# GLA recurrence and squared-ReLU MLP in one kernel: which queue loads blocks 3 and 4, and the order of the opening

## Chip, core and metric

One core of one Trainium2 chip. The metric is the device time of one execution in microseconds (us). Differences are judged by medians of runs on the same chip.

## The reference

For each of 4 batches and 8 heads a state of 48 x 48 is carried over 768 steps: it decays by alpha, takes the outer product of k and v, and is read with q. The heads' outputs, side by side, are the 384 columns of x (3072 rows), which go through a squared-ReLU layer of width 2048.

```python
for t in range(S):
    state = alpha[:, :, t, :, None] * state + einsum('bhd,bhe->bhde', k[:, :, t], v[:, :, t])
    y[:, :, t] = einsum('bhd,bhde->bhe', q[:, :, t], state)
x = y.transpose(0, 2, 1, 3).reshape(B * S, H * D)
r = maximum(x @ w_in, 0)
out = (s * (r * r) + b) @ w_out
```

## The kernel before

The rows of x are cut into 24 blocks of 128 (six for each batch). Block n needs four loads (alpha, k, q, v; 192 KB each, in runs of 192 bytes), and then passes these steps. The names are those of the kernel's functions, and blocks are counted from 0, so that the "third and fourth block" are numbers 2 and 3.

- `ln` (L203, ScalarE): logarithm of alpha.
- `cum` (L210, TensorE; L221 and L222, ScalarE): cumulated sum by a triangular matrix, then two exponentials, the inverse decay and the decay. For the first five blocks a third, small exponential (L224) gives the block's total decay. From block 6 on the total decay goes through DRAM instead (`decay`, L230 and L232): one row is written out and read back, by SyncE's DMA queue.
- `vcast` (L206, GpSimd): v to bf16.
- `qk` (L238, L239, VectorE, also DVE): the products k times inverse decay and q times decay.
- `tr` (L244, TensorE; L249, VectorE): transposes of both, and their copy out of PSUM.
- `amat` (L259, TensorE; L267, VectorE): q times k for each head, written to the two PSUM tiles `a_ps`, and then masked.
- `yp` (L278, L287, L298, TensorE; L305, ScalarE): y from the carried state and from the block itself, the block's share of the next state, and y to bf16. `st` (L334 VectorE, L339 and L343 GpSimd) brings the state forward.
- `xt` (L312, TensorE; L318, ScalarE): y transposed, the layer's input.
- `mp(g, u)` (L365, TensorE): a quarter u of the hidden units of block g, 12 matmuls. It writes one of two PSUM tiles `h_ps` in turn, or `o_ps` where (g, u) is listed in `h_in_o` (L351). `rl` (L379, ScalarE) is its relu, `sq` (L386, VectorE) its square. `mr` is mp and rl; `m` is mp, rl and sq.
- `o(g, u)` (L402, TensorE): a quarter of the second matmul, four matmuls that add up over u = 0 to 3. Block 1 adds up in the first tile of `a_ps`, block 2 in the second one, all others in `o_ps`. Behind u = 3 the sum of an early block is copied to a store in SBUF (L411, ScalarE), since the bias is not ready yet.

The weights come by DMA as four quarters each of w_in (768 KB) and w_out. `win(i)` turns a quarter of w_in to bf16 (L154 ScalarE, L156 VectorE). `wout(i)` does so for w_out: quarters 1 and 3 on VectorE (L160), quarter 2 on ScalarE (L168), quarter 0 half and half. `colsum` (L175, L177, VectorE) adds up w_out for the bias.

Nothing is scheduled by the compiler. Each engine runs its instructions in the order in which the program issues them, and that order is a list sorted by position: the opening (L512 to L527) is written out by hand, from `(ln, 0)` to the attention matmuls of block 4; later blocks have positions by formula (L541 on). `busy` (L191) puts matmuls without use on TensorE in the opening; they write `o_ps`.

The loads are issued ahead of the list: blocks 0 and 1 by SyncE, then the quarters of w_in with two loads each of blocks 2 and 3 between, then w_out, then blocks 4 to 7. Two more loads each of blocks 2 and 3 are issued by ScalarE, in its own DMA queue, where the list has `early` (L492).

Of the kernel before, what the change touches and what calls it, by code (L numbers as in the profile page):

```python
# [14 lines left out]
def kernel(  # L15
# [12 lines left out]
    nc = tc.nc  # L28
# [88 lines left out]
    def src(t, n):  # L117
        b, c = n // NCH, n % NCH
        return t[b, :, c * C : (c + 1) * C, :].rearrange("h s d -> s h d")

    def load_a(n, eng=None):
        (eng or nc.sync).dma_start(out=al_sb[n % NLD], in_=src(alpha, n))

    def load_q(n, eng=None):
        (eng or nc.sync).dma_start(out=q_sb[n % NLD], in_=src(q, n))

    def load_k(n, eng=None):
        (eng or nc.sync).dma_start(out=k_sb[n % NLD], in_=src(k, n))

    def load_v(n, eng=None):  # L130
        (eng or nc.sync).dma_start(out=v_sb[n % NLD], in_=src(v, n))
# [8 lines left out]
    def load_w_in(i):  # L140
        cols = slice(i * d_ff // 4, (i + 1) * d_ff // 4)
        nc.sync.dma_start(
            out=w_in_st[:, :, cols], in_=moe_w_in[:, cols].rearrange("(t r) f -> r t f", t=KT)
        )
# [203 lines left out]
    nrelu = [0]  # L348


    h_in_o = {(1, 3), (2, 2)}  # L351
    h_of = {}

    def mp(g, u):
# [94 lines left out]
    quarter = d_ff // 4  # L449
    load_w_in(0)  # L450
    load_w_in(1)
    load_q(2)
    load_v(2)
    load_w_in(2)
    load_w_in(3)
    load_q(3)
    load_v(3)
    for j in range(0, NJ, 4):
        load_w_out(j, j + 4)
    for n in range(4, NLD):  # L460
# [17 lines left out]
    def at(pos, fn, *args):  # L478
        events.append((pos, len(events), fn, args))
# [10 lines left out]
            cast_w_out(4 * i, 4 * i + 4, i == 2)  # L490

    def early(n):  # L492
        load_a(n, nc.scalar)
        load_k(n, nc.scalar)

    def win(i):
        cast_w_in(i * quarter, (i + 1) * quarter, int(i < 3))
# [14 lines left out]
    for pos, what in enumerate(  # L512
        [
            (ln, 0), (vcast, 0), (cum, 0), (qk, 0), (spread,), (busy, 3), (tr, 0), (busy, 1), (ln, 1), (vcast, 1), (amat, 0),
            (cum, 1), (early, 2), (busy, 3), (yp, 0), (qk, 1), (st, 0), (busy, 1), (tr, 1), (xt, 0), (busy, 2), (amat, 1),
            (win, 0), (win, 1), (busy, 5), (yp, 1), (mr, 0, 0), (st, 1), (busy, 1), (xt, 1), (ln, 2), (early, 3), (mr, 0, 1),
            (sq, 0, 0), (cum, 2), (sq, 0, 1), (m, 1, 0), (mr, 1, 1), (vcast, 2), (qk, 2), (sq, 1, 1), (busy, 4), (tr, 2),
            (win, 2), (busy, 3), (amat, 2), (busy, 1), (mr, 0, 2), (mr, 1, 2), (yp, 2), (win, 3), (st, 2), (sq, 0, 2),
            (sq, 1, 2), (busy, 2), (ln, 3), (xt, 2), (mr, 0, 3), (cum, 3), (mr, 1, 3), (vcast, 3), (qk, 3), (mr, 2, 0),
            (sq, 0, 3), (mr, 2, 1), (mr, 2, 2), (tr, 3), (sq, 1, 3), (mr, 2, 3), (sq, 2, 0), (wout, 0), (amat, 3),  # L520
            (busy, 3), (o, 0, 0), (yp, 3), (sq, 2, 1), (st, 3), (sq, 2, 2), (sq, 2, 3), (wout, 1), (o, 1, 0), (xt, 3),
            (o, 2, 0), (m, 3, 0), (m, 3, 1), (wout, 2), (o, 0, 1), (o, 1, 1), (colsum, 1), (ln, 4), (m, 3, 2), (m, 3, 3),
            (wout, 3), (o, 2, 1), (cum, 4), (o, 0, 2), (vcast, 4), (qk, 4), (o, 1, 2), (o, 2, 2), (colsum, 2), (o, 0, 3),
            (o, 1, 3), (o, 2, 3), (tr, 4), (o, 3, 0), (amat, 4),
        ]
    ):
        at(0.1 * pos, *what)  # L527
# [63 lines left out]
```

## Time and profile before

| what | value |
|---|---|
| median of 3 runs (range) | 197.93 us (197.66 to 198.06) |
| profiled execution | 197.71 us |
| its span, first to last instruction | 195.9 us |
| mean granted TensorE clock | 1.00 |
| VectorE, ScalarE, GpSimd busy | 151.6, 118.6, 62.1 us |
| TensorE idle until its first matmul | 4.5 us |
| DMA, mean over the span | 155 GB/s |
| transposes of blocks 2, 3, 4 start | 22.14, 30.88, 45.56 us |
| attention matmuls of block 4 start | 47.03 us |

A line of a timeline gives the start in us from the span's beginning, the duration, the engine, the line of the kernel, output and inputs with their shapes, how many instructions are merged, and in brackets how long the engine had been idle and what ended that. Matmuls are pipelined: a merged row lasts longer than the distance to the next one. "issue" in the chain is time in which the engine waited for nothing that the profile shows.

### The profile page before, as it was taken

Reading aid. Unit: us, or ns where it says so; the run is one execution under the profiler, and the core shown is the slowest. Engines: PE = TensorE matmul, PEld = TensorE weight load, DVE = VectorE, ACT = ScalarE, POOL = GpSimd, SP = SyncE. Lnnn points to the kernel's source line nnn. Section 1 sums busy time; section 2 is a strip of 40 time slices with the busy share of each in tenths; the row PEclk is TensorE's granted clock in tenths of the full one; section 3 lists DMA queues with packets and bytes.
Section 4 is the critical chain, followed back from the end, with each engine's and each line's share of the span. In section 5 each row is a group of like instructions: output and inputs, shape, how many; then the busy total and the mean of one; then the engine's idle time right before and its main releaser. Section 6 shows DMA issues by size and latency. Waiting matters only on the chain.

```text
span 195.9 us, 6122 instructions
## 1 busy us (share of the span) xinstructions
PE 183.2 (94%) x2441; PEld 143.4 (73%) x2441; DVE 151.6 (77%) x296; ACT 118.6 (61%) x243; POOL 62.1 (32%) x96
## 2 busy tenths in 40 slices
PE   0979798999899999999999999999999999999994
PEld 0547486775767678778878877887877877877783
DVE  5486779886577597988977996989887999998532
ACT  3256486565767566676586676675675666654650
POOL 5143141511310074524500650531701752652000
PEclk9999999999999999999999999999999999999999
DMA  6999999999999546845968569549849563332202
GB/s 122 191 338 225 325 268 372 208 191 192 174 195 160 111 78 94 158 85 85 202 124 141 96 93 161 100 88 253 164 122 208 103 147 124 85 120 84 93 31 80
DMA packets 113454, 30.33 MB, mean 155 GB/s; under 512 B 106627, under 2 KB 111890, under 8 KB 113426
## 3 DMA queue, kind: packets, MB, share of 16 engines
q1 hardware_dynamic: 109262, 29.15, 73.5%
q10 hardware_dynamic: 4164, 0.79, 2.8%
q8 instruction: 19, 0.31, 0.7%
q14 instruction: 9, 0.07, 0.1%
HBM read 25.19 MB, written 4.74 MB: 153 GB/s over the span
## 4 chain that ended last, share of the span: by engine, by line
PE 76%; DMA 8%; DVE 7%; ACT 4%; issue 3%; SPq 0%; ACTq 0%; DVEq 0%
PE h_ps L365 26%; PE o_ps L402 26%; PE ct_ps L244 6%; DMA k_sb<-in_k_dram 6%; PE a_ps L259 3%; PE a_ps L402 3%; PE y_ps L287 2%; ACT r_sb L379 2%; DVE qkT L249 2%; PE ct_ps L210 2%; PE h_ps L312 2%; DMA al_sb<-in_alpha_dram 2%; DVE qb_sb L239 2%; PE y_ps L278 1%; PE p_ps L298 1%
## 5 line engine op out<-in xcount | busy, mean ns | idle before, releaser
L379 ACT ACTIVATE r_sb<-h_ps 128x512 bf16<-128x512 f32 x94 | 55.8, 597 | 39.1 <-PE h_ps L365 37.4
L365 PE MATMUL h_ps<-xd_all,w_in_bf 128*128 128x128 bf16 x1128 | 74.6, 219 | 0.7 <-ACT xd_all L318 0.3
L365 PEld LDWEIGHTS <-w_in_bf 128*128 128x128 bf16 x1152 | 69.2, 98 | 7.2 <-issue 1.1
L402 PE MATMUL o_ps<-w_out_bf,gt_all 128*128 128x384 bf16 x336 | 68.5, 326 | 0.3 <-ACT w_out_bf L168 0.2
L386 DVE TENSOR_TENSOR gt_all<-r_sb 128x512 bf16<-128x512 bf16 x96 | 45.0, 480 | 26.5 <-ACT r_sb L379 25.8
L339 POOL TENSOR_TENSOR sd_sb<-t_sb,blast 48x192 bf16<-48x192 f32 x40 | 21.6, 539 | 100.2 <-DVE t_sb L334 62.7
L402 PEld LDWEIGHTS <-gt_all 128*128 128x128 bf16 x368 | 32.5, 98 | 16.3 <-issue 0.5
L206 POOL CAST v_bf<-v_sb 128x384 bf16<-128x384 f32 x24 | 18.0, 756 | 16.0 <-DMA v_sb<-in_v_dram 13.2
L318 ACT ACTIVATE xd_all<-h_ps 128x384 bf16<-128x384 bf16 x24 | 11.7, 489 | 14.8 <-PE h_ps L312 14.8
L343 POOL TENSOR_TENSOR sc_sb<-t_sb,blast 112x384 f32<-112x384 f32 x16 | 20.2, 1265 | 1.3
L249 DVE COPY qkT<-ct_ps 112x1024 bf16<-112x1024 bf16 x24 | 16.4, 683 | 4.2 <-PE ct_ps L244 2.9
L238 DVE TENSOR_TENSOR kb_sb<-k_sb,bi_sb 128x384 bf16<-128x384 f32 x24 | 14.8, 617 | 5.3 <-ACT bi_sb L221 3.7
L239 DVE TENSOR_TENSOR qb_sb<-q_sb,b_sb 128x384 bf16<-128x384 f32 x24 | 16.9, 706 | 1.5 <-ACT b_sb L222 1.5
L267 DVE TENSOR_TENSOR am_a<-a_ps,mask 128x512 bf16<-128x512 f32 x24 | 16.4, 682 | 1.8 <-PE a_ps L259 1.8
L267 DVE TENSOR_TENSOR am_b<-a_ps,mask 128x512 bf16<-128x512 f32 x24 | 16.3, 679 | 0.0
L203 ACT ACTIVATE la_sb<-al_sb 128x384 bf16<-128x384 f32 x24 | 12.4, 517 | 4.0 <-DMA al_sb<-in_alpha_dram 4.0
L221 ACT ACTIVATE bi_sb<-ct_ps 128x384 f32<-128x384 f32 x24 | 11.7, 487 | 4.1 <-PE ct_ps L213 2.3
L244 PEld LDWEIGHTS <-qb_sb 128*112 128x112 bf16 x96 | 8.0, 132 | 7.5 <-DVE qb_sb L239 6.5
L305 ACT ACTIVATE y_bf<-y_ps 128x384 bf16<-128x384 f32 x24 | 11.7, 487 | 2.3 <-PE y_ps L287 2.3
L222 ACT ACTIVATE b_sb<-ct_ps 128x384 f32<-128x384 f32 x24 | 11.9, 494 | 1.6 <-DMA row_dr<-b_sb 1.6
L210 PE MATMUL ct_ps<-la_sb,U_bf 128*128 128x384 bf16 x24 | 8.0, 333 | 4.7 <-ACT la_sb L203 4.7
L244 PE MATMUL ct_ps<-ident,qb_sb 128*112 128x128 bf16 x96 | 10.1, 228 | 2.1 <-DVE qb_sb L239 1.9
(66 smaller groups left out, 191.1 us busy)
## 6 DMA issues: line engine op xcount, KB each, us to landing
q_sb<-in_q_dram SPq DMA_DIRECT2D x24, 192.0 KB, 4.1
v_sb<-in_v_dram SPq DMA_DIRECT2D x24, 192.0 KB, 4.2
al_sb<-in_alpha_dram SPq DMA_DIRECT2D x22, 192.0 KB, 3.0
k_sb<-in_k_dram SPq DMA_DIRECT2D x22, 192.0 KB, 4.1
w_in_st<-in_moe_w_in_dram SPq DMA_DIRECT2D x4, 768.0 KB
w_out_st<-in_moe_w_out_dram SPq DMA_DIRECT2D x4, 768.0 KB
out_dram<-w_in_st SPq DMA_DIRECT2D x13, 192.0 KB, 3.6
out_dram<-out_sb SPq DMA_DIRECT2D x10, 192.0 KB, 3.5
```

Source lines behind the costliest of these rows:

```text
L206: nc.gpsimd.tensor_copy(out=v_bf[n % 3], in_=v_sb[n % NLD])
L238: nc.vector.tensor_tensor(out=kb_sb[n % 3][:, :, 0:48], in0=k_sb[n % NLD], in1=bi_sb[n % 2], op=ALU.mult)
L239: nc.vector.tensor_tensor(out=qb_sb[n % 2][:, :, 0:48], in0=q_sb[n % NLD], in1=b_sb[n % 2], op=ALU.mult)
L244: nc.tensor.transpose(out=t_ps[0:112, x, p, :], in_=t.rearrange("a h d -> a (h d)")[:, 128 * p : 128 * p + 112], identity=ident,)
L249: nc.vector.tensor_copy(out=qkT_sb[n % 2][0:112].rearrange("a x p t -> a (x p t)"), in_=t_ps[0:112].rearrange("a x p t -> a (x p t)"),)
L267: nc.vector.tensor_tensor(out=am_sb[e][n % 2], in0=a_ps[e], in1=mask4, op=ALU.mult)
L339: nc.gpsimd.tensor_tensor(out=sd[r, :, d], in0=t1_sb[r, :, d], in1=bl[r].to_broadcast([48, NP, 48]), op=ALU.mult)
L343: nc.gpsimd.tensor_tensor(out=sc_sb[0:112], in0=t1_sb[0:112], in1=bl[0:112].to_broadcast([112, NP, 96]), op=ALU.mult)
L365: nc.tensor.matmul(out=hp[:, jj * N : (jj + 1) * N], lhsT=w_in_bf[:, kk, 128 * j : 128 * (j + 1)], rhs=xd_sb[g][:, kk, 0:N], start=(kk == ...
L379: nc.scalar.activation(out=rs, in_=h_of.pop((g, u)), func=AF.Relu)
L386: nc.vector.tensor_tensor(out=gt_sb[g][:, u * 512 : (u + 1) * 512], in0=rs, in1=rs, op=ALU.mult)
L402: nc.tensor.matmul(out=op[:, 0:d_model], lhsT=gt_sb[g][:, j * N + t * C : j * N + (t + 1) * C], rhs=w_out_bf[:, j, :], start=(j == 0), sto ...
```

## The change

Three things change. SyncE loads alpha and k of blocks 2 and 3 where it loaded q and v; ScalarE's `early` loads q and v where it loaded alpha and k. The opening's list has another order from `(early, 3)` on: `cum` and `qk` of block 2 and 3 stand ahead of some relus (`rl`) and squares (`sq`), for which mp, rl and sq are now listed apart; w_out's casts, the column sum and the last `o` quarters stand elsewhere; 28 filler matmuls in place of 29. The two groups that write `o_ps` are (2, 0) and (0, 3), formerly (1, 3) and (2, 2).

```diff
-    h_in_o = {(1, 3), (2, 2)}
+    h_in_o = {(2, 0), (0, 3)}
...
-    load_q(2)
-    load_v(2)
+    load_a(2)
+    load_k(2)
     load_w_in(2)
     load_w_in(3)
-    load_q(3)
-    load_v(3)
+    load_a(3)
+    load_k(3)
...
     def early(n):
-        load_a(n, nc.scalar)
-        load_k(n, nc.scalar)
+        load_q(n, nc.scalar)
+        load_v(n, nc.scalar)
...
-            (win, 0), (win, 1), (busy, 5), (yp, 1), (mr, 0, 0), (st, 1), (busy, 1), (xt, 1), (ln, 2), (early, 3), (mr, 0, 1),
-            (sq, 0, 0), (cum, 2), (sq, 0, 1), (m, 1, 0), (mr, 1, 1), (vcast, 2), (qk, 2), (sq, 1, 1), (busy, 4), (tr, 2),
-            (win, 2), (busy, 3), (amat, 2), (busy, 1), (mr, 0, 2), (mr, 1, 2), (yp, 2), (win, 3), (st, 2), (sq, 0, 2),
-            (sq, 1, 2), (busy, 2), (ln, 3), (xt, 2), (mr, 0, 3), (cum, 3), (mr, 1, 3), (vcast, 3), (qk, 3), (mr, 2, 0),
-            (sq, 0, 3), (mr, 2, 1), (mr, 2, 2), (tr, 3), (sq, 1, 3), (mr, 2, 3), (sq, 2, 0), (wout, 0), (amat, 3),
-            (busy, 3), (o, 0, 0), (yp, 3), (sq, 2, 1), (st, 3), (sq, 2, 2), (sq, 2, 3), (wout, 1), (o, 1, 0), (xt, 3),
-            (o, 2, 0), (m, 3, 0), (m, 3, 1), (wout, 2), (o, 0, 1), (o, 1, 1), (colsum, 1), (ln, 4), (m, 3, 2), (m, 3, 3),
-            (wout, 3), (o, 2, 1), (cum, 4), (o, 0, 2), (vcast, 4), (qk, 4), (o, 1, 2), (o, 2, 2), (colsum, 2), (o, 0, 3),
-            (o, 1, 3), (o, 2, 3), (tr, 4), (o, 3, 0), (amat, 4),
+            (win, 0), (win, 1), (busy, 5), (yp, 1), (mr, 0, 0), (st, 1), (busy, 1), (xt, 1), (ln, 2), (early, 3), (mp, 0, 1),
+            (sq, 0, 0), (cum, 2), (rl, 0, 1), (mr, 1, 0), (vcast, 2), (qk, 2), (sq, 0, 1), (mr, 1, 1), (busy, 1), (tr, 2),
+            (sq, 1, 0), (busy, 3), (amat, 2), (win, 2), (busy, 5), (yp, 2), (st, 2), (busy, 1), (xt, 2), (mr, 0, 2), (win, 3),
+            (mp, 1, 2), (ln, 3), (rl, 1, 2), (mp, 2, 0), (sq, 1, 1), (cum, 3), (rl, 2, 0), (vcast, 3), (sq, 0, 2), (mr, 2, 1),
+            (qk, 3), (sq, 1, 2), (mr, 2, 2), (mr, 0, 3), (tr, 3), (mr, 1, 3), (sq, 2, 0), (mr, 2, 3), (amat, 3), (sq, 2, 1),
+            (wout, 0), (busy, 2), (yp, 3), (st, 3), (o, 0, 0), (xt, 3), (sq, 0, 3), (sq, 1, 3), (o, 1, 0), (sq, 2, 2),
+            (sq, 2, 3), (m, 3, 0), (wout, 1), (o, 2, 0), (m, 3, 1), (m, 3, 2), (wout, 2), (o, 0, 1), (m, 3, 3), (o, 1, 1),
+            (ln, 4), (wout, 3), (colsum, 1), (o, 2, 1), (cum, 4), (o, 0, 2), (vcast, 4), (qk, 4), (o, 1, 2), (o, 2, 2),
+            (tr, 4), (o, 1, 3), (colsum, 2), (o, 2, 3), (amat, 4), (o, 0, 3), (o, 3, 0),
```

## The prediction

> **What bounds the kernel now.** I read the page first, then the granted clock by stage, then the chain of waits, then each engine's timeline from 16 to 70 us. The profiled execution took 197.71 us: a span of 195.9 us and 1.8 us around it. The median of the three runs is 197.93 us; the sum is made against 197.71 and 0.2 us is added at the end.
>
> From the page: TensorE (PE) is busy 94% of the span; in the second fence line each digit is a slice of 4.9 us, and behind the first five PE has two eights and, at the end, a 4; all else is 9. The DMA row is at 9 for slices 2 to 13, to about 64 us.
>
> ```profile
> PE 183.2 (94%) x2441; PEld 143.4 (73%) x2441; DVE 151.6 (77%) x296; ACT 118.6 (61%) x243; POOL 62.1 (32%) x96
> ...
> PE   0979798999899999999999999999999999999994
> ...
> DMA  6999999999999546845968569549849563332202
> ```
>
> Part of that opening PE time is filler (`busy`). So in the opening the bound is read from what PE waits for. The timelines give three waits on inputs: block 2's v, block 3's alpha and block 3's k.
>
> ```profile
> 19.85 0.50 POOL L206 CAST v_bf<-v_sb 128x384 bf16<-128x384 f32 x1 [0.43 <-DMA v_sb<-in_v_dram]
> ...
> 26.87 0.52 ACT L203 ACTIVATE la_sb<-al_sb 128x384 bf16<-128x384 f32 x1 [0.20 <-DMA al_sb<-in_alpha_dram]
> ...
> 29.06 1.30 DVE L238 TENSOR_TENSOR kb_sb<-k_sb,bi_sb 128x384 bf16<-128x384 f32 x1 [1.41 <-DMA k_sb<-in_k_dram]
> ```
>
> (start, duration, engine, line, then in brackets the idle time and what ended it.) After 36 us PE has almost no gap until the first decay row, which sits in SyncE's queue behind all loads up to block 10. The chain of waits shows that place:
>
> ```profile
> 64.26 2.69 DMA row_dr<-b_sb
> ...
> 67.03 0.50 ACT b_sb L222
> ...
> 67.56 0.57 DVE qb_sb L239
> ...
> 68.17 0.65 PE ct_ps L244 x8
> ```
>
> PE had finished its earlier work 0.38 us before 68.17 (its timeline row says 0.38 <-DVE qb_sb). So a loss of up to 0.38 us before that point is free, and no gain before it reaches the end unless the DMA stream also gets shorter. After it PE is dense and later blocks are in the old order: a delay there goes to the end in full.
>
> **Part 1, the queues.** Alpha and k of blocks 2 and 3 take the places in SyncE's queue that q and v had, and q and v take theirs on ScalarE. All are 192 KB in the same shape, and the number of DMAs per queue is the same; nothing passes another load. So I take each landing from the row of the load it replaces: alpha(2) as q(2), k(2) as v(2), 19.8 us (the cast row); alpha(3) as q(3); k(3) as v(3), whose issue at 17.62 plus 11.6 us to landing gives 29.2. In the other queue alpha(3) landed at 26.8 and k(3) at 28.96. q's landings are not shown. Packet counts by queue show both queues in step (15.0 to 18.0 us: 1564 of ScalarE's, 1554 of SyncE's), so I put alpha(2) at 17.6 (its old issue 9.97 + 7.6) and alpha(3) at 26.8; bounds are -1 and +1 us. The change of queue alone is worth about 0: k(3), which ended the longest wait, lands 0.2 us later.
>
> **Part 2, block 2.** The exponentials go ahead of a relu, the products ahead of a square. Old: they ran at 19.28, behind the relu of 18.79. New: cumulation still at 18.35, +0.53 to the first exponential, 18.88 to 19.37; k's product waits for k(2), 19.85; q's product ends 20.9. The relu moved behind now ends 20.29, and the fourth product group needs its buffer, so PE waits 0.9 us more there (19.4 to 20.33), then 0.67 + one filler 0.22: transposes at 21.22, against 22.14. With copy (0.69), attention matmuls, masks (0.61 apart, 0.68), block 2's y ends at 24.8 instead of 26.0.
>
> **Part 3, block 3.** What was gained runs into alpha(3): logarithm at 26.95, cumulation 27.64, exponentials 28.17 to 29.04, relu of (2,0) to 29.58, then (0,3), which shares o_ps with it, 29.62 to 30.29. k's product starts at 29.25; it took 1.30 us when GpSimd ran beside it and 0.55 otherwise; I take 0.7, between (q's product of block 1 took 0.85 beside one cast). Transposes at 30.45 (30.3 to 30.9), against 30.88. After them (1,3) and (2,3), 1.34; attention matmuls 32.24; second mask done 34.01; y needs it, and only two fillers (0.43) lie between, so PE idles 0.85 and y ends at 34.41, against 35.13. But o(0,0), formerly ahead of y, now follows, with 0.2 waiting for DVE's weight cast. When both orders have done o(0,0), y, x's transposes and o(1,0), before stands at 35.95 and after at 36.08: **+0.13**, one filler (0.22) fewer included.
>
> **Part 4, the tail of the opening list.** Here the after's order exposes waits. Intervals: twelve matmuls 0.67, four of the o kind 0.65, matmul group to relu 0.88, relu to square 0.63, four o matmuls to the start of their copy 0.85, copy 0.49 + 0.05. The rows:
>
> ```profile
> 38.72 1.57 ACT L168 ACTIVATE w_out_bf<-w_out_st,sb_col 128x1536 bf16<-128x1536 f32 x1
> ...
> 39.50 0.95 DVE L175 TENSOR_TENSOR cs_sb<-w_out_st 128x768 f32<-128x768 f32 x1
> ...
> 42.05 1.26 DVE L160 TENSOR_SCALAR w_out_bf<-w_out_st,sb_col 128x1536 bf16<-128x1536 f32 x1
> ...
> 44.46 0.49 ACT L411 ACTIVATE w_in_st<-o_ps 128x384 f32<-128x384 f32 x1 [1.69 <-PE o_ps L402]
> ...
> 45.76 0.49 ACT L411 ACTIVATE w_in_st<-a_ps 128x384 f32<-128x384 f32 x1 [0.16 <-PE a_ps L402]
> ```
>
> (a) m(3,0) starts at 36.17 (0.1 wait, as before). DVE's cast of the second quarter of w_out now stands behind its square: relu 37.05 to 37.65, square, cast 38.02 to 39.28. o(0,1) starts at 39.33 where PE was free at 38.83: 0.5.
> (b) m(3,2) at 38.16, relu 39.04, then ScalarE's cast of the third quarter (1.47 to the next) stands ahead of the relu of (3,3): 41.0 to 41.62. Logarithm of block 4 follows, cumulation 42.07, 0.1 idle. DVE: square 41.65, last cast 42.0, and the column sum, which formerly ran at 39.5 in a gap, now 43.2 to 44.1 ahead of the products: 44.0 and 44.5 to 45.06. Transposes of block 4 at 45.1; PE, with three o's after the cumulation, was free at 44.35: 0.75.
> (c) o(1,3) 45.55, o(2,3) 46.2, then at once the attention matmuls of block 4, which write the two a_ps that hold o(1) and o(2). The second copy runs at 46.2 + 0.85 = 47.05 to 47.54, so seven of eight matmuls wait: end 47.9, where 46.85 + 0.33 = 47.18 was possible: 0.72.
> (d) o(0,3) 47.9, copy at 48.75 to 49.24, and o(3,0) follows in the same o_ps with nothing between: starts 49.29 instead of 48.55, 0.74. Before had two o's and the transposes there.
>
> New waits: 0.1 + 0.5 + 0.1 + 0.75 + 0.72 + 0.74 = 2.9. Old waits in this stretch, now inside them: 0.1 before m(3,0) and 0.37 before the attention matmuls (46.66 to 47.03) = 0.47. o(3,0) and the attention matmuls are both done at 49.94, against 47.36: 0.13 + 2.9 - 0.47 = **+2.6 us**. (c) and (d) are orders on one buffer and surest; (a) and (b) rest on one place in a queue each, and a gain at 30.45 of up to 0.15 or a loss of 0.45 shifts all.
>
> **From there to the end.** The order is the old one, so its own waits (0.35 before m(4,0), 0.3 before y of block 5) stay. At 67.8 + 2.6 = 70.4 PE no longer meets the decay row's gate, and 0.38 is saved: +2.6 - 0.4 = **+2.2 us**, 199.9 beside this execution, 200.1 beside the median.
>
> **A rule weighed.** Granted clock 1.00 is printed throughout, yet PE's fillers are 0.42 us apart at 5.7 us and 0.215 apart from 9.8 us on. Behind the 1.01 us gap that ended at 22.14 they stay at 0.215. The Trainium skill, "TensorE: Matmul & The Clock Gate", Part 1, says that the array falls to half clock after an idle window of about 3.4 us; by that rule gaps of 0.5 to 0.9 us cost nothing more. Its section "A second HAM failure mode: psum-queue depth-cycling" says that frequent micro-idling between groups can also bring the half clock, and speaks against this change. No run here shows that yet.
>
> **Rivals.**
> 1. Some of the cover that I miss exists: DVE or ScalarE reach (a) and (b) earlier, or parts overlap. Then only (c) and (d) remain, 1.46, less 0.47 and 0.38, with the 0.13: +0.7, 198.7 us (198.3 to 199.2). For: in before, wide copies ran beside others without loss. Against: each chain hangs on one instruction in a strict order.
> 2. Neutral: the opening's lead of 0.7 us at block 3's y (34.41 against 35.13) is larger than I think, and pays for the tail. PE must be at block 8's transposes by 68.17, so the lead must reach some 2.2 us; then 197.9. Against: (0,3) behind the relu of (2,0) holds the transposes at 30.3 at the earliest.
> 3. Faster: SyncE's stream closes one of its holes. DMA is nearly empty at 37 to 39, at 53 and at 62.2 to 63.5 us. If ScalarE's pair, moved by an earlier or later logarithm, removes the last one (1.3 us), the row lands near 65.7, the gate of 0.38 opens, and with no tail waits a filler (0.22) comes off too: 197.3. It decides when the row lands ahead of 66.6 and PE is on time. Against: ScalarE's packets of block 3 move only from 22 us whatever the issue time (18.1), so the stream should not change.
> 4. The half clock comes back over the tail's gaps: as at the start, some 4.9 us (4.5 to 9.4) at half rate, at most 2.4 us more: up to 202.5.
>
> **How the numbers follow.** Forecast 58% (199.2 to 200.9); rival 1, 16%; neutral 9%; faster 10%; half clock 7%. The time is the likeliest case's, 200.1. For 8 in 10 the range leaves out the half clock's far end and the faster case, and reaches into rival 1: 198.4 to 201.1. About 0.2% (0.4 us) is what a measurement can tell from no change. Slower 58 + 16 + 7 = 81%, same 9%, faster 10%.
>
> **What would show it.** Right: transposes of block 2 near 21.2 and of block 3 near 30.45; PE idle 0.7 each before block 4's attention matmuls (ended by ScalarE's copy, L411), before o(3,0) (the same) and before block 4's transposes; no wait on b_sb near 67. Wrong: k(3) landing far from 29.2; block 4's transposes before 44.5; PE at block 8's transposes before 68.6; fillers or groups at twice their spacing.

## The result, and the profile after

The changed kernel is slower. Its median of 6 executions is 200.23 us (199.54 to 202.27), that of before in the same runs 198.0 us (197.66 to 198.35). The ratio is 1.0128, with a 95% interval of 1.0081 to 1.0175. The forecast was 200.1 us. The profiled execution took 199.99 us with a span of 198.2 us, 2.3 us more than the span of before. Ratios leave out a few executions far above the others of the same kernel.

The page of after: TensorE's row has eights in slices 9 to 11 (39 to 54 us), where before has 9, 9 and 8; the DMA row is at 9 over slices 2 to 13 as before.

```profile
PE   1999899988899999999999999999999999999994
...
DMA  7999999999999384693968846958947953122212
```

The lines that answer to the three waits on inputs, from the timelines of ScalarE, VectorE and GpSimd: in this execution none of them waits for a DMA any more, not even the product with k(3), at 29.64 us, which waits for its exponential.

```profile
20.32 0.50 POOL L206 CAST v_bf<-v_sb 128x384 bf16<-128x384 f32 x1
```

```profile
27.88 0.52 ACT L203 ACTIVATE la_sb<-al_sb 128x384 bf16<-128x384 f32 x1
```

```profile
20.34 0.89 DVE L238 TENSOR_TENSOR kb_sb<-k_sb,bi_sb 128x384 bf16<-128x384 f32 x1 [1.24 <-ACT bi_sb L221]
...
29.64 0.56 DVE L238 TENSOR_TENSOR kb_sb<-k_sb,bi_sb 128x384 bf16<-128x384 f32 x1 [1.13 <-ACT bi_sb L221]
```

TensorE's timeline shows where the time went. In brackets is its idle time and what ended it: product groups (0,1) and (1,1), then block 3's y, w_out's second cast, block 4's transposes, and the two waits for copies out of PSUM (L411). The last line is block 8's transposes, which wait for nothing.

```profile
18.51 0.83 PE L365 MATMUL h_ps<-xd_all,w_in_bf 128*128 128x128 bf16 x12 [0.30 <-ACT r_sb L379]
...
21.29 0.83 PE L365 MATMUL h_ps<-xd_all,w_in_bf 128*128 128x128 bf16 x12 [0.82 <-ACT r_sb L379]
...
34.91 0.20 PE L287 MATMUL y_ps<-v_bf,am_b 128*128 128x48 bf16 x1 [0.40 <-DVE am_b L267]
...
38.32 1.50 PE L365 MATMUL h_ps<-xd_all,w_in_bf 128*128 128x128 bf16 x24
40.48 0.81 PE L402 MATMUL o_ps<-w_out_bf,gt_all 128*128 128x384 bf16 x4 [0.66 <-DVE w_out_bf L160]
...
44.09 1.46 PE L402 MATMUL a_ps<-w_out_bf,gt_all 128*128 128x384 bf16 x8
45.84 0.43 PE L244 MATMUL ct_ps<-ident,qb_sb 128*112 128x128 bf16 x4 [0.29 <-DVE qb_sb L239]
...
48.37 0.38 PE L259 MATMUL a_ps<-qkT 48*128 48x128 bf16 x7 [0.42 <-ACT w_in_st L411]
48.68 0.82 PE L402 MATMUL o_ps<-w_out_bf,gt_all 128*128 128x384 bf16 x4
50.09 1.46 PE L402 MATMUL o_ps<-w_out_bf,gt_all 128*128 128x384 bf16 x8 [0.58 <-ACT w_in_st L411]
...
70.90 0.39 PE L244 MATMUL ct_ps<-ident,qb_sb 128*112 128x128 bf16 x4
```

The bracketed number can be smaller than the gap: the idle time is counted behind the modelled end of the matmul before. The distance between starts is surer: o(0,3) at 48.68 takes 0.65, so o(3,0) could have started at 49.33; it started at 50.09, 0.76 later. In the same way o(0,1) could have started at 39.66 (the 24 matmuls from 38.32 on take 1.34) and waited 0.82, and block 4's transposes at 45.39 (eight matmuls from 44.09 on take 1.30) and waited 0.45.

Lined up, the two profiled executions differ like this:

| point | before | after | difference | added since |
|---|---|---|---|---|
| group (0,1) starts (same order up to here) | 17.55 | 18.51 | +0.96 | +0.96 |
| o(0,0), y, x of block 3, o(1,0) all done | 35.95 | 36.91 | +0.96 | 0.00 |
| o(3,0) and attention matmuls of block 4 done | 47.36 | 50.74 | +3.38 | +2.42 |
| transposes of block 8 | 68.17 | 70.90 | +2.73 | -0.65 |
| span | 195.9 | 198.2 | +2.3 | -0.4 |

The first 0.96 us lies ahead of everything that the change reorders, and is a longer start at half rate. In TensorE's timeline the fillers (three or two in a row) are 0.42 us apart, then 0.215; in before the three at 9.79 run at the short distance, in after the three at 9.97 still at the long one.

Before:

```profile
7.83 0.63 PE L193 MATMUL o_ps<-mask,U_bf 128*128 128x512 bf16 x1
...
9.79 0.81 PE L193 MATMUL o_ps<-mask,U_bf 128*128 128x512 bf16 x3
```

After:

```profile
9.97 1.44 PE L193 MATMUL o_ps<-mask,U_bf 128*128 128x512 bf16 x3
...
13.44 1.06 PE L193 MATMUL o_ps<-mask,U_bf 128*128 128x512 bf16 x2
```

The profile of `gate_off` below, which has before's opening, has the long start too (three fillers in 1.44 us at 10.05), so it isn't the change's.

Not all of such a start reaches the end. In `gate_off` group (0,1) starts 0.58 us later than in before (18.13), and block 3's transposes at 30.88 as in before: the start went into the wait for k(3), which that profile doesn't have. So before would have kept 0.38 of the 0.96, and the 0.00 in the second row of the table hides a loss at the changed head: from the start of group (0,1) to the end of o(1,0) and x it takes 18.40 us in after and 17.83 in `gate_off`.

The Trainium skill, "TensorE: Matmul & The Clock Gate", Part 1, says that the window over which activity is judged runs free of the kernel's start, so that the moment of the rise differs between executions; these profiles agree, with 0.96 us between two.

### The profile page after: what moved, and what is told of

Same layout as the page of the kernel before. It is cut to its first block, busy times and chain, and to the rows that moved or that the text cites. A ratio compares the mean times of both kernels' runs of the same rounds, so it can differ in the third digit from the quotient of the medians.

```text
span 198.2 us, 6120 instructions
## 1 busy us (share of the span) xinstructions
PE 185.2 (93%) x2440; PEld 145.3 (73%) x2440; DVE 150.8 (76%) x296; ACT 118.8 (60%) x243; POOL 64.2 (32%) x96
## 4 chain that ended last, share of the span: by engine, by line
PE 68%; SPq 15%; DMA 10%; DVE 3%; ACT 1%; issue 1%; ACTq 0%; DVEq 0%
PE h_ps L365 25%; PE o_ps L402 25%; DMA q_sb<-in_q_dram 8%; SPq L128 5%; PE ct_ps L244 5%; SPq L147 4%; PE a_ps L259 3%; SPq L125 3%; SPq L122 2%; PE ct_ps L210 2%; PE y_ps L287 2%; PE h_ps L312 2%; DMA al_sb<-in_alpha_dram 2%; SPq L131 1%; PE a_ps L425 1%; PE y_ps L278 1%
## 5 line engine op out<-in xcount | busy, mean ns | idle before, releaser
L339 POOL TENSOR_TENSOR sd_sb<-t_sb,blast 48x192 bf16<-48x192 f32 x40 | 22.5, 563 | 103.5 <-DVE t_sb L334 67.3
L343 POOL TENSOR_TENSOR sc_sb<-t_sb,blast 112x384 f32<-112x384 f32 x16 | 21.8, 1362 | 1.3
L238 DVE TENSOR_TENSOR kb_sb<-k_sb,bi_sb 128x384 bf16<-128x384 f32 x24 | 13.7, 569 | 8.3 <-ACT bi_sb L221 8.2
L244 PEld LDWEIGHTS <-qb_sb 128*112 128x112 bf16 x96 | 8.5, 136 | 4.4 <-DVE qb_sb L239 3.2
L259 PE MATMUL a_ps<-qkT 48*128 48x128 bf16 x192 | 10.2, 226 | 1.0 <-DVE qkT L249 0.4
```

What stands on the lines that cost most here:

```text
L244: nc.tensor.transpose(out=t_ps[0:112, x, p, :], in_=t.rearrange("a h d -> a (h d)")[:, 128 * p : 128 * p + 112], identity=ident,)
L259: nc.tensor.matmul(out=a_ps[e][:, p, :], lhsT=qkT[r0 : r0 + 48, 1, p, :], rhs=qkT[r0 : r0 + 48, 0, p, :], start=True, stop=True,)
L339: nc.gpsimd.tensor_tensor(out=sd[r, :, d], in0=t1_sb[r, :, d], in1=bl[r].to_broadcast([48, NP, 48]), op=ALU.mult)
L343: nc.gpsimd.tensor_tensor(out=sc_sb[0:112], in0=t1_sb[0:112], in1=bl[0:112].to_broadcast([112, NP, 96]), op=ALU.mult)
```

## The experiments

The theory: the loss is made in the tail of the opening's list, by waits for casts and copies, and a gate at block 8 (a DMA row) hides part of it. The rivals: the swap of the queues; the head of the list; the clock. All ratios are to before, run on the same chip.

**Queues or order.** The two parts of the change, one at a time. `queues_only` is before with the four load lines and `early` changed; `order_only` has the new list and `h_in_o`, with before's loads.

```diff
# queues_only, on before
-    load_q(2)
-    load_v(2)
+    load_a(2)
+    load_k(2)
...
-        load_a(n, nc.scalar)
-        load_k(n, nc.scalar)
+        load_q(n, nc.scalar)
+        load_v(n, nc.scalar)
```

> Before's order, with the changed queues alone. Theory (the loss is made in the order of the opening's tail): 197.7 to 198.3 us, the landings of alpha and k of blocks 2 and 3 within 0.5 us of those of before. Rival (the swap of the queues costs, because k(3) now sits behind w_in in SyncE's queue): 199 to 200.2 us, with k(3) awaited past 29.5 us.

Measured: 198.19 us, ratio 0.9996 (0.9979 to 1.0012). The swap of the queues costs nothing that shows. In its profile k(3) lands 11.0 us behind its issue at 18.1, at 29.1 us, and nothing waits for it.

> The changed order and o_ps groups, with before's queues. Theory: all of the loss, 199.6 to 200.9 us, with the waits before o(0,1), before the attention matmuls of block 4 and before o(3,0) as in the changed kernel. Rival (queues cost): 198 to 198.5 us.

Measured: 200.71 us, ratio 1.0139 (1.0094 to 1.0184). The order is the whole loss.

**Head or tail.** The new list is cut behind the squares of (2,3). `tail_old` is the changed kernel with before's list from there, `tail_new` is before with the new list from there (w_out's second cast moves with it).

```diff
# tail_old, on the changed kernel; tail_new has the reverse on before
-            (sq, 2, 3), (m, 3, 0), (wout, 1), (o, 2, 0), (m, 3, 1), (m, 3, 2), (wout, 2), (o, 0, 1), (m, 3, 3), (o, 1, 1),
-            (ln, 4), (wout, 3), (colsum, 1), (o, 2, 1), (cum, 4), (o, 0, 2), (vcast, 4), (qk, 4), (o, 1, 2), (o, 2, 2),
-            (tr, 4), (o, 1, 3), (colsum, 2), (o, 2, 3), (amat, 4), (o, 0, 3), (o, 3, 0),
+            (sq, 2, 3), (wout, 1),
+            (o, 2, 0), (m, 3, 0), (m, 3, 1), (wout, 2), (o, 0, 1), (o, 1, 1), (colsum, 1), (ln, 4), (m, 3, 2), (m, 3, 3),
+            (wout, 3), (o, 2, 1), (cum, 4), (o, 0, 2), (vcast, 4), (qk, 4), (o, 1, 2), (o, 2, 2), (colsum, 2), (o, 0, 3),
+            (o, 1, 3), (o, 2, 3), (tr, 4), (o, 3, 0), (amat, 4),
```

> The changed kernel up to the squares of (2,3), then before's tail of the opening, from w_out's second cast on. Theory: the loss is gone, 197.7 to 198.4 us, since at o(1,0) both kernels stand level and the gate of block 8 hides 0.4 us. Rival (the opening's head loses, by its relus that hold up the product groups): 199.5 us or more.

Measured: 198.21 us, ratio 1.0006 (0.9980 to 1.0033).

> Before's order up to the transposes of x of block 3, then the changed tail from m(3,0) on. Theory: the changed tail's 2.4 us, some 0.6 more because m(3,0) now waits for x of block 3 with no o between, less 0.5 at the gate: 200.5 us (199.8 to 201.2). Rival (the head loses): 198 to 198.7 us.

Measured: 200.96 us, ratio 1.0131 (1.0100 to 1.0161). The tail alone makes the loss, and the head alone makes none that reaches the end. In the profile of `tail_old` the head does cost: block 4's transposes come 27.92 us behind group (0,1), in `gate_off`, with nearly the same start, 27.44. At block 8 that profile waits for the DMA row (ScalarE 1.31 us), which hides it.

**Which waits of the tail.** `sums_early` is to take away what I called (a) and (b), `copies_covered` (c) and (d), `both_mended` does both. In `copies_covered` o(0,3) also comes ahead of block 4's transposes and covers most of (b): 0.11 us of wait is left there (48.87 to 48.98).

```diff
# sums_early, on the changed kernel
-(sq, 2, 3), (m, 3, 0), (wout, 1), (o, 2, 0), (m, 3, 1), (m, 3, 2),
+(sq, 2, 3), (wout, 1), (m, 3, 0), (o, 2, 0), (m, 3, 1), (colsum, 1), (m, 3, 2),
...
-(ln, 4), (wout, 3), (colsum, 1),
+(ln, 4), (wout, 3),
# copies_covered, on the changed kernel
-(tr, 4), (o, 1, 3), (colsum, 2), (o, 2, 3), (amat, 4), (o, 0, 3), (o, 3, 0),
+(o, 0, 3), (tr, 4), (o, 1, 3), (colsum, 2), (o, 2, 3), (o, 3, 0), (amat, 4),
```

> The changed kernel with w_out's second cast ahead of m(3,0) and the first column sum ahead of m(3,2), so that neither stands behind a late square. Theory (the four waits of the tail add up): the wait before o(0,1), 0.66 us in the profile, goes and block 4's transposes come 0.9 us earlier: 199.4 us against the 200.3 us of the changed kernel's median (198.8 to 199.9). Rival (the two copies that o_ps and a_ps wait for take the gain back): no gain, 200 to 200.6 us.

Measured: 200.18 us (198.88 to 201.67), ratio 1.0107 (1.0067 to 1.0146). That is above the range I gave. In its profile, whose group (0,1) starts within 0.04 us of after's, block 4's transposes start at 45.25 instead of 45.84 and no longer wait, and block 8's at 70.27 instead of 70.90: 0.6 us, not 0.9, because the cumulation now waits for block 4's logarithm, behind ScalarE's cast:

```profile
42.96 0.32 PE L210 MATMUL ct_ps<-la_sb,U_bf 128*128 128x384 bf16 x1 [0.43 <-ACT la_sb L203]
...
45.25 0.39 PE L244 MATMUL ct_ps<-ident,qb_sb 128*112 128x128 bf16 x4
...
47.74 0.38 PE L259 MATMUL a_ps<-qkT 48*128 48x128 bf16 x7 [0.42 <-ACT w_in_st L411]
...
49.45 1.46 PE L402 MATMUL o_ps<-w_out_bf,gt_all 128*128 128x384 bf16 x8 [0.58 <-ACT w_in_st L411]
```

Both copies are still awaited there, as before the mend. The ratio's interval overlaps that of the changed kernel, so the times alone don't show the 0.6.

> The changed kernel with o(0,3) ahead of block 4's transposes and o(3,0) ahead of its attention matmuls, so that each copy out of PSUM runs beside other matmuls. Theory: o(3,0) and the attention matmuls done at 48.9 instead of 50.7 us of the profile, so 1.8 us less: 198.5 us (198.0 to 199.1). Rival (the two waits only move to the mask of block 4 and to y): 199.5 us or more.

Measured: 198.4 us, ratio 1.0031 (1.0006 to 1.0056). Two places moved in the list give back three quarters of the loss.

> Both mends together, queues and head as in the changed kernel. Theory: 200.3 - 1.8 - 0.9 = 197.6, but the gate of block 8 stops the gain near 68.2 us, so 197.8 us (197.4 to 198.3), no faster than before. Rival (no gate): 197.3 us or less.

Measured: 198.63 us, ratio 1.0025 (0.9998 to 1.0053): 0.3 us above the range, and no better than `copies_covered`. Its profile shows the gate. TensorE could start block 8's transposes at 68.13 (four matmuls from 67.48 on take 0.65) and starts them at 68.91. The first row is block 7's:

```profile
62.32 0.43 PE L244 MATMUL ct_ps<-ident,qb_sb 128*112 128x128 bf16 x4
...
68.91 0.43 PE L244 MATMUL ct_ps<-ident,qb_sb 128*112 128x128 bf16 x4 [0.61 <-DVE qb_sb L239]
```

So the second mend's gain ends at the DMA row, here at 68.91 where before had 68.17; when the row lands is not the same in every execution.

**The gate by itself.** `gate_off` is before, with the total decay of block 6 made by four small matmuls and an exponential, as blocks 0 to 4 have it. So the first row through DRAM is block 7's.

```diff
# gate_off, on before
-        if n < NCH - 1:
+        if n < NCH - 1 or n == NCH:
             for p in range(NP):
...
-        if n < NCH - 1:
+        if n < NCH - 1 or n == NCH:
             nc.scalar.activation(out=blast[n % 3][0:112, :, 0], in_=tot_ps[0:112], func=AF.Exp)
```

> Before, with block 6's total decay by the small matmuls of blocks 0 to 4 instead of through DRAM, so that no DMA row is awaited at block 8. Theory (that row holds TensorE for 0.38 us at 68.17): the wait goes, 0.17 us of small matmuls come: 0.2 to 0.5 us less than before, 197.7 us. Rival (the wait is only moved to the next row or the next block): as before or 0.1 us more.

Measured: 197.31 us, ratio 0.9956 (0.9930 to 0.9982), faster than both kernels, by more than I gave. ScalarE's timeline shows the cause. Block 8's decay goes into the one of the two buffers `b_sb` out of which block 6's row is written. So in before the second exponential of block 8 waits 1.57 us for the row, and the relus behind it with it:

```profile
64.98 0.49 ACT L221 ACTIVATE bi_sb<-ct_ps 128x384 f32<-128x384 f32 x1
67.03 0.49 ACT L222 ACTIVATE b_sb<-ct_ps 128x384 f32<-128x384 f32 x1 [1.57 <-DMA row_dr<-b_sb]
67.42 1.08 ACT L379 ACTIVATE r_sb<-h_ps 128x512 bf16<-128x512 f32 x2
```

In `gate_off` they follow each other:

```profile
65.21 0.49 ACT L221 ACTIVATE bi_sb<-ct_ps 128x384 f32<-128x384 f32 x1
65.58 0.50 ACT L222 ACTIVATE b_sb<-ct_ps 128x384 f32<-128x384 f32 x1
66.74 1.27 ACT L379 ACTIVATE r_sb<-h_ps 128x512 bf16<-128x512 f32 x2 [0.66 <-PE h_ps L365]
```

The two profiled spans differ by 0.5 us (195.9 and 195.4), as expected; why the medians differ by 0.95 us isn't shown. Rows that land later in other executions of before (67.0 us here; 67.6 in `mended_gate`) would do it.

**The clock.** In the profile of `order_only` group (1,1) waits 1.78 us, until 21.82, instead of 0.82, and then everything runs at half rate. By the granted clock in slices of 1 us (columns: slice, length, then each engine's busy time; PEclk stands ahead of the last two):

```profile
21.00:22.00 1.00, 0.18 (x4) 0.17 (x4) 1.00 (x3) 1.00 (x4) 0.00 (x0) 1.00 1.04 385
22.00:23.00 1.00, 1.00 (x13) 0.82 (x11) 0.24 (x1) 0.41 (x2) 0.00 (x0) 0.68 1.08 344
23.00:24.00 1.00, 1.00 (x10) 0.97 (x9) 0.00 (x0) 0.96 (x2) 0.00 (x0) 0.50 1.31 256
24.00:25.00 1.00, 1.00 (x4) 0.19 (x2) 0.87 (x2) 0.00 (x0) 0.00 (x0) 0.50 1.44 198
25.00:26.00 1.00, 1.00 (x10) 0.46 (x10) 0.21 (x2) 0.00 (x0) 0.00 (x0) 0.62 1.46 188
```

ScalarE's timeline names what made the gap longer: the issue of its second load of block 3 took 1.56 us (0.61 in after), and the exponentials now stand right behind it.

```profile
18.30 0.52 ACT L203 ACTIVATE la_sb<-al_sb 128x384 bf16<-128x384 f32 x1
18.69 1.56 ACTq L128 DMA_DIRECT2D k_sb<-in_k_dram  x1
20.35 0.49 ACT L221 ACTIVATE bi_sb<-ct_ps 128x384 f32<-128x384 f32 x1 [1.53 <-PE h_ps L365]
```

Three more profiles have such a long issue. In `copies_covered` (1.82 us) the gap is 2.06 us, and the granted clock is 0.50 from 24.0 to 27.4 us. In `tail_new` (1.55) and `queues_only` (1.40), which have before's head, the relu of (0,1) stands ahead of the exponentials; the gap is 0.87 and 0.77 us, and the granted clock stays at 1.00. So the long issue isn't the change's, but the changed order lets it open the gap.

Two runs try this: `gap_filled` covers the gap by four fillers (the texts on record count three), `early_late` issues the two loads later.

```diff
# gap_filled, on the changed kernel
-(sq, 0, 1), (mr, 1, 1), (busy, 1),
+(sq, 0, 1), (busy, 4), (mr, 1, 1), (busy, 1),
# early_late, on the changed kernel
-(ln, 2), (early, 3), (mp, 0, 1),
+(ln, 2), (mp, 0, 1),
...
-(rl, 0, 1), (mr, 1, 0),
+(rl, 0, 1), (early, 3), (mr, 1, 0),
```

> The changed kernel with three fillers more (0.65 us) between the product groups (1,0) and (1,1), where TensorE waits for the relu of (0,1), 0.82 us in one profile and 1.78 us in another. Theory (this gap lets the granted clock fall in some executions): the fillers cost nothing, every execution has a granted clock of 0.998 or more, and the median falls to 199.6 to 200.2 us with the slowest below 200.8. Rival (the clock falls for other reasons): some executions at 0.99 and up to 202 us as before, median 200.3 or more.

Measured: 200.28 us (199.95 to 201.27), ratio 1.0118 (1.0095 to 1.0142). No execution under 0.998, but the median didn't fall, and the slowest was above 200.8.

> The changed kernel with ScalarE's two loads of block 3 issued behind the exponentials and the relu of (0,1), not ahead of them. Theory (in two profiles ScalarE took 1.56 and 1.82 us for the second issue instead of 0.6, with the exponentials behind it, and the granted clock fell in the gap): the exponentials start 0.5 us behind the cumulation in every execution, none has a granted clock below 0.998, median 199.6 to 200.2 us. Rival (the ordinary gap of 0.8 us is enough): executions at 0.99 remain, median 200.3 us or more.

Measured: 199.97 us (199.56 to 201.66), ratio 1.0099 (1.0065 to 1.0132), no execution under 0.999. In its profile the exponentials start at 20.30, 0.51 us after the cumulation (19.79), and the two issues come at 20.32 and 22.30.

Each of the two runs had only 6 executions. Counted over all runs with the changed head and without these mends (the changed kernel, `order_only`, `tail_old`, `sums_early`, `copies_covered`, `both_mended`), 10 of 54 executions had a mean granted clock of 0.989 to 0.992. With before's head (before, `queues_only`, `tail_new`, `gate_off`) it was 2 of 105; with one or both mends (also `mended_gate`, `mended_free`), 1 of 36. Chance alone would bring two counts as far apart as 10 of 54 and 1 of 36 in about 1 case of 20: that the mends work is likely, and not shown. The six executions of `order_only` give the price: 202.1 and 202.8 us with the low clock, 199.85 to 200.8 without.

**A better version.** `mended_gate` has the changed queues and head, both of these mends and before's tail. w_out's first cast is moved up, so that o(0,0) takes the place of two fillers. `mended_free` adds the edit of `gate_off`.

```diff
# mended_gate, on tail_old (with the edits of gap_filled and early_late)
-(tr, 3), (mr, 1, 3),
+(tr, 3), (wout, 0), (mr, 1, 3),
...
-            (wout, 0), (busy, 2), (yp, 3), (st, 3), (o, 0, 0), (xt, 3), (sq, 0, 3), (sq, 1, 3), (o, 1, 0), (sq, 2, 2),
+            (o, 0, 0), (yp, 3), (st, 3), (o, 1, 0), (xt, 3), (sq, 0, 3), (sq, 1, 3), (sq, 2, 2),
```

> The changed queues and head, with before's tail; further, ScalarE's loads of block 3 behind the relu of (0,1), three fillers in the gap ahead of (1,1), and w_out's first cast ahead of (1,3), so that o(0,0) takes the place of two fillers. Theory: TensorE is 0.7 us ahead of before at x of block 3, but the DMA row's gate at block 8 takes it back: 197.8 to 198.3 us, with a wait on the decay of block 8 of 0.5 to 1 us. Rival (no gate): 197.4 us or less.

Measured: 197.95 us, ratio 0.9987 (0.9965 to 1.0009): no difference, as expected. The row held ScalarE for 1.20 us; TensorE's own wait of 0.5 to 1 us did not come, since this execution was late already at block 1's x (18.03, against 16.92 in before): ScalarE's last cast of w_in ahead of it waited for its DMA until 16.96, in before until 15.73.

> The kernel of the run mended_gate, with block 6's total decay by matmuls as in gate_off. Theory: the lead of 0.7 us and the 0.4 us of the gate both reach the end, less 0.17 us: 197.1 us (196.8 to 197.5), faster than both kernels. Rival (the lead is lost elsewhere): 197.7 us or more.

Measured: 197.57 us, ratio 0.9969 (0.9954 to 0.9984). It beats both kernels, but not `gate_off`: the lead of 0.7 us did not reach the end. The profiles show why. I had measured it against the profiled execution of before, which waited for k(3). From group (0,1) to block 3's transposes it took 13.33 us there (17.55 to 30.88), but 12.75 in `gate_off` (18.13 to 30.88), whose late start hid that wait, and 12.74 in after and here (18.24 to 30.98). So where the start is long, before's head loses nothing against the changed one, and the lead at m(3,0) is 0.25 us (36.56 - 18.24 against 36.70 - 18.13). o(0,1) then starts 0.49 us later than it could (37.90 to 38.39), waiting for w_out's second cast, and at block 4's transposes nothing is left (27.68 against 27.44).

## Why the prediction was right

**The tail, step by step.** The working gave +2.45 us between o(1,0) and o(3,0); measured +2.42. (c) is 0.72 as forecast (matmuls done at 48.68, o(2,3) at 47.63, 0.33 of work), (d) 0.76 for 0.74. (a) and (b) were both mis-sized, and the two errors cancel by luck: (a) is 0.82 for 0.5, since w_out's second cast took 1.58 us and not 1.26; (b) is 0.45 for 0.75, mostly because TensorE came there later by what (a) had cost more. `copies_covered` confirms the size of (c) and (d) with most of (b) (198.4 us for 198.5).

**The queues and the head.** About 0 for the queues was right (`queues_only`). The waits for k(2) and k(3), on which the working for blocks 2 and 3 rests, are not in after's profile: its long start brings the exponentials later than the loads. `both_mended` has the changed queues and head and a short start, and there VectorE waits as worked out:

```profile
19.77 0.63 DVE L238 TENSOR_TENSOR kb_sb<-k_sb,bi_sb 128x384 bf16<-128x384 f32 x1 [1.90 <-DMA k_sb<-in_k_dram]
...
29.13 0.70 DVE L238 TENSOR_TENSOR kb_sb<-k_sb,bi_sb 128x384 bf16<-128x384 f32 x1 [1.43 <-DMA k_sb<-in_k_dram]
```

Forecast were 19.85 and 29.2; block 2's transposes come at 21.37 (forecast 21.22), block 3's at 30.58 (30.45), and o(1,0) and x are done at 36.24 (36.08), against 35.95 in before. So the head's +0.13 is +0.29 with a short start, and with a long one 0.57 (18.40 against 17.83), because there is then no wait for k(3) in before that could be saved.

**The gate.** Forecast 0.38 saved; 0.65 at block 8, and 0.4 more by the end. The 0.38 was read from the bracket; by starts before waits 0.54 there (four matmuls from 66.98 on take 0.65, so 67.63 against 68.17), and the other 0.1 lies between block 5's and block 6's transposes (6.12 us in before, 6.03 in after). Behind 67 us TensorE's weight loads waited for q's products 2.4 us in all in before and 0.9 us in after, which is where the 0.4 would come from; that was not tried by itself.

**What the sum did not have.** The 2.3 us between the two profiles are 0.38 that before would have kept of the longer start, 0.58 at the head and 2.42 in the tail, less 0.65 at the gate and 0.43 behind it. The sum had 0.13, 2.45 and 0.38 saved. What it lacked on the one side nearly balances what it lacked on the other, so the agreement of 200.1 with 200.23 is better than the terms are.

**The rivals.** Rival 1 is out: (a) and (b) came, 1.27 us in sum for 1.25. So is rival 2: no lead of the opening paid for the tail. Rival 4, the half clock, exists, though the place was another: not the tail's gaps but the one before group (1,1), when ScalarE's issue lengthens it. I had priced ScalarE's issues at nothing, and they stand in its strict order ahead of the exponentials. Rival 3's holes in the DMA stream did not matter, but its gate did: opened from the other side, it made before faster.

Of the rules weighed, the tail's gaps of 0.3 to 0.8 us came with a granted clock of 1.00 in every slice of `order_only` from 30 us on, and the fall came behind gaps of 1.78 and 2.06 us (`order_only`, `copies_covered`). The Trainium skill, "TensorE: Matmul & The Clock Gate", section "A second HAM failure mode: psum-queue depth-cycling", says that frequent micro-idling between groups can bring the half clock; the tail does not bear it out. The idle window of about 3.4 us that the Trainium skill names in Part 1 of the same page is longer than these gaps; the clock fell all the same, and the measurement decides.

## What to carry to other kernels

Walk an order written by hand buffer by buffer: a result that is copied out of a PSUM tile, followed at once by work that writes the same tile, costs the latency of matmul and copy (here 0.85 + 0.54 us, of which 0.65 is the matmuls' own time), and another group moved between them takes it away (`copies_covered`). Read such waits from the distance between starts: the brackets were up to 0.2 us too small. Before you value a gain or a loss, find the next place where a stream that doesn't hear of the change (a DMA queue) sets the time: it swallows gains, absorbs losses, and can be the better thing to remove. An engine that issues DMAs holds what is queued behind them, so don't put the critical exponentials there. Before you line up two profiles, look whether their starts are alike, and whether a wait for a load takes up the difference.

## What the runs showed of the hardware

- The issue of ScalarE's second load of block 3 (192 KB) took 0.59 to 0.62 us in nine of the fourteen profiles (0.37 in `early_late`, where it comes later), but 1.40 to 1.82 us in four (`queues_only`, `tail_new`, `order_only`, `copies_covered`), and the engine started nothing else meanwhile. In these four the issue of its second load of block 2 was slow too (1.00 to 1.73). What makes it long isn't settled.
- The granted clock fell to 0.50 about half a microsecond behind the end of a gap of 1.78 us, and for 3.4 us: by the slices of `order_only` 0.64 + 1 + 1 + 0.76 us at half rate, so 1.7 us of work lost. In `copies_covered` it fell 1.1 us behind the end of a gap of 2.06 us (22.93 to 24.0), and again for 3.4 us.
- The same cast of w_out by VectorE (128 x 1536) took 1.01 us where GpSimd did nothing (after, 42.96), 1.26 where GpSimd's cast of v ran beside it for 0.44 (before, 42.05), 1.58 where GpSimd's step of the state (L343) did for 0.77 (after, 38.84), and 2.03 where both did, for 1.22 in all (`order_only`, 40.77). That GpSimd is the cause was not tried by itself.
- The rise to the full rate at the start came between 7.8 and 9.8 us in before, and between 13.4 and 15.0 us in after, with the same instructions on TensorE up to there; the page's row of granted clocks prints 9 for both.
